# DeltaNet and SwiGLU on one core: where a chunk's first gate/value product stands, and which engine issues the output stores

## Chip, core and metric

The kernel runs on one core of a Trainium2 chip. The metric is the device time of one execution in microseconds (us). All arithmetic is in fp32.

The engines named below are TensorE (PE in the profile; PEld is its weight load), VectorE (DVE), ScalarE (ACT), GpSimd (POOL) and SyncE (SP). SP does no arithmetic. It issues DMA transfers, and ACT can issue them too. Each engine runs its own instructions in the order in which they were emitted, and engines wait for one another by semaphores.

## What is computed

The reference chains two blocks. The first is a DeltaNet recurrence over 768 time steps for 4 batches and 8 heads of size 48; the second is a SwiGLU feed-forward layer on its output, with 3072 tokens, a model width of 384 and an inner width of 1536:

```python
for t in range(S):
    y[:, :, t] = einsum('bhd,bhde->bhe', q[:, :, t], state)
    v_old = einsum('bhde,bhd->bhe', state, k_n[:, :, t])
    state = state + beta_t * einsum('bhd,bhe->bhde', k_n[:, :, t], v[:, :, t] - v_old)
x = y.transpose(0, 2, 1, 3).reshape(B * S, H * D)
g, val = x @ w_gate, x @ w_val
out = (g * sigmoid(g) * val) @ w_out
```

`k_n` is k divided by its norm.

## The kernel before

**Tiling.** Time is cut into 12 chunks of 64 steps. A chunk has 64 steps of 4 batches, so 256 tokens for the feed-forward layer. For each chunk the heads' part (the recurrence: Gram matrices, a triangular inverse, four steps of `advance`) makes the tile `xts[c]`, the layer's input; the feed-forward part of chunk c then runs while the heads' part of chunk c + 1 is put in between in small pieces.

**Order.** The order is written out by hand: inside `manual_schedule` all five engines keep the order of emission. `point(c + 1)` is a *head visit*: it emits one piece of the heads' work, which is either a step of `advance`, a join of the inverse, or the Gram products of a later chunk. `fill(n)` emits some n us of VectorE work of the inverse, with now and then a ScalarE copy (line 698). `finish(c + 1)` emits what is still missing of the next chunk's `advance`, and `x_sums` emits four small VectorE sums of the new input.

**Two forms of the feed-forward layer.** Chunks 0 to 2 use plain products (`gate_val`, line 1009, and `output`, line 1038). Chunks 3 to 11 (`c >= FAST`, with `FAST = 3`) use a form with seven block products instead of eight, in three rounds per chunk (`gate_val_fast`, matmuls at line 928) and one `output_fast` (line 1125). It works in four PSUM banks, called `p_x`, `p_w`, `p_y` and `p_v`.

**How a round begins.** `begin` makes a first product into `p_x` on PE (eight matmul records in the trace) and copies it to `p_y` on ACT (line 945). Then a second product goes into `p_w`, with ACT copying `p_w` away (line 971), and a third product is accumulated onto `p_y`. That third product needs ACT's copy at line 945 to have ended. Then ACT copies `p_y` to `p_v` (line 974). For rounds 1 and 2 `begin` is emitted at the end of the round before. For round 0 it stands inside round 0, after the head visit that the loop over chunks emits at line 1439:

```python
point(c + 1)                         # head visit
if c >= FAST:
    for r in range(ROUNDS):
        gate_val_fast(c, r, fill)    # round 0: begin(0), then product(p_w ...)
```

**Stores.** Each half of a chunk's output lies in a tile `o_sb`, of which there are two, and is stored by two DMAs of 96 KB (line 1055). ACT issues them for chunks 0 to 2, SP for chunks 3 to 11. All other loads of this part of the kernel are issued by SP: k, q and v of later chunks (lines 136, 169, 183), and the kept sums of weights (line 941). The loads by `first_blocks` are emitted between the two `output` calls of chunk 1, after the store of its first half.

Of the kernel before, what the change touches and what calls it, by code (L numbers as in the profile page):

```python
# [20 lines left out]
def kernel(  # L21
# [25 lines left out]
    nc = tc.nc  # L47
# [21 lines left out]
    def ps_pair(name, tag):  # L69
# [3 lines left out]
    ffn_banks = [  # L73
        psum.tile([128, 512], FP32, name=f"ffn{i}", tag=f"ffn{i}", bufs=1)
        for i in range(4)
    ]
    taken = []

    def ps_ffn(shape, name, bank=None):
        if bank is None:  # L80
            taken.append(name)
            bank = (len(taken) - 1) % 4
        n = 1
        for m in shape[1:]:
            n *= m
        p = ffn_banks[bank][:, 0:n]
        return p if len(shape) == 2 else p.rearrange("p (x n) -> p x n", x=shape[1])
# [240 lines left out]
    kt, qt, a_sb, a_of, p_sb, xts = {}, {}, {}, {}, {}, {}  # L328
# [3 lines left out]
    def half_of(x):  # L332
        return slice(64 * x, 64 * x + 64)
# [522 lines left out]
    def new_h(c, f, at):  # L856
        hs[c, f] = hp[at].rearrange("p (i n) -> p i n", i=2)
# [5 lines left out]
    def units(t):  # L863
        return t.rearrange("p (u n) -> p u n", u=4)

    w_s = {1: units(hp[6]), 2: units(hp[7]), 4: units(p_places[0][:, 0:512])}
# [6 lines left out]
    x_t = const.tile([128, 3, 128], FP32, name="x_t")  # L873

    def w_pair(m, t, f):
        return (wg_sb, wv_sb)[m][:, t, 128 * f : 128 * f + 256].rearrange(
            "p (i n) -> p i n", i=2
        )
# [31 lines left out]
    def x_sums(c):  # L910
        if c < NCH and c not in summed and steps("advance", c) >= 4:
            summed.add(c)
            sums_of_x(c)

    ROUNDS = 3

    def gate_val_fast(c, r, fill):

        f1, f2 = 2 * r, 2 * r + 6
        x = xts[c]  # L920
        p_x, p_w, p_y, p_v = (
            units(ps_ffn([128, 512], "p_gate", bank)) for bank in range(4)
        )
        tok = slice(0, 128), slice(128, 256)

        def product(p, w, moving, start=False):
            for u in range(4):
                nc.tensor.matmul(  # L928
                    p[:, u], w(u), moving, start=start and u == 0, stop=True,
                    skip_group_check=True,  # L930
                )

        def plain(t, f):
            return lambda u: w_pair(u // 2, t, f)[:, u % 2]

        def summed_w(n):
            return lambda u: w_s[n][:, u]

        def next_sums(n):
            if c < NCH - 1 or r < ROUNDS - 1:  # L940
                nc.sync.dma_start(out=w_s[n], in_=kept[n, (r + 1) % ROUNDS])

        def begin(r):
            product(p_x, plain(0, 2 * r), x[:, 0, tok[0]], True)
            nc.scalar.copy(p_y, p_x)  # L945

        def silu(p, n):
            nc.scalar.activation(  # L948
                sil[:, n].rearrange("p (i n) -> p i n", i=2), p[:, 0:2], ACTF.Silu
            )  # L950

        def times(p, n, f, j):
            nc.vector.tensor_tensor(  # L953
                out=h_of(c, f, j),
                in0=sil[:, n].rearrange("p (i n) -> p i n", i=2),
                in1=p[:, 2:4],
                op=ALU.mult,
            )

        def combo_or_fill(n):  # L960
            if combos:
                combos.pop(0)()
                n -= 1.9
            fill(n)

        for f in (f1, f2):
            new_h(c, f, f // 2)
        if r == 0:
            begin(0)
        product(p_w, summed_w(1), x_t[:, 0], True)  # L970
        nc.scalar.copy(m5, p_w)
        next_sums(1)
        product(p_y, summed_w(2), x_t[:, 1])
        nc.scalar.copy(p_v, p_y)  # L974
        next_sums(2)
        product(p_x, plain(1, f1), x[:, 1, tok[0]])
        product(p_x, plain(2, f1), x[:, 2, tok[0]])
        plus(p_y, p_y, m5)
        product(p_v, plain(0, f2), x[:, 0, tok[1]])
        silu(p_x, 0)  # L980
        fill(1)
        times(p_x, 0, f1, 0)
        plus(p_w, p_v, m5)
        point_and_fill(c + 1, 3.4, combo_or_fill)
        product(p_y, summed_w(4), x[:, 1, tok[1]])
        next_sums(4)
        product(p_y, plain(2, f1), x[:, 2, tok[1]])
        silu(p_y, 1)
        times(p_y, 1, f1, 1)
        product(p_w, plain(2, f2), x[:, 2, tok[1]])  # L990
        silu(p_w, 0)
        times(p_w, 0, f2, 1)
        product(p_v, plain(1, f2), x_t[:, 2])
        product(p_v, plain(2, f2), x[:, 2, tok[0]])
        silu(p_v, 1)
        sums_of_h(c, f2)
        times(p_v, 1, f2, 0)
        if r < ROUNDS - 1:
            begin(r + 1)
        point_and_fill(c + 1, 5, combo_or_fill)  # L1000

    def gate_val(c, f, fill, within=None, behind=None):
# [49 lines left out]

    def store(c, bp, o_sb):
        for b in range(2):
            (nc.scalar if c < FAST else nc.sync).dma_start(
                out=out_v[2 * bp + b, c * C : (c + 1) * C],
                in_=o_sb[half_of(b)],
            )
# [3 lines left out]
    FAST = 3  # L1062
# [18 lines left out]
    def plus(out, a, b):  # L1081
        nc.vector.tensor_tensor(out=out, in0=a, in1=b, op=ALU.add)  # L1082
# [12 lines left out]
    def h_of(c, f, bp):  # L1095

        return hs[c, f][:, :, 128 * bp : 128 * bp + 128]
# [6 lines left out]
    def sums_of_h(c, f):  # L1104
        f1 = f - FH
        nc.vector.tensor_tensor(
            out=s_of(1, f1), in0=h_of(c, f1, 1), in1=h_of(c, f, 1), op=ALU.add
        )
        minus(s_of(2, f1), s_of(1, f1), h_of(c, f1, 0))
        minus(h_of(c, f1, 1), h_of(c, f1, 0), h_of(c, f1, 1))  # L1110
# [71 lines left out]
    def step(kind, fn, *args):  # L1182
        key = (kind, args or (1,))
        if key not in gens:
            gens[key] = [fn(*args), 0]
        next(gens[key][0], None)
        gens[key][1] += 1

    def steps(kind, *args):
        return gens.get((kind, args), (None, 0))[1]  # L1190
# [33 lines left out]
    def may_advance(c):  # L1224
        g = c // 2
        due = {0: 1, 1: 2 + 2 * (c % 2)}.get(g, 2)
        return steps("advance", c) > 0 or (c in p_sb and steps("join", g) >= due)
# [12 lines left out]
    def prep_step(c):  # L1240

        if first:
            first.pop(0)()
            return True
        for g in range(1, c // 2 + 2):
            late = g == 1 and (
                hold or steps("join", g) >= 2 and steps("advance", 2) < 4
            )
            if g in inverted and steps("join", g) < (4 if g == 1 else 2) and not late:
                step("join", join if g > 1 else join_1, *((g,) if g > 1 else ()))  # L1250
                return True
        if going:
            next(going.pop())
            return True
        k_c, q_c = None, None
        if q_of and steps("advance", q_of[0] - 1) >= 3:
            q_c = q_of.pop(0)
        elif not (c > 0 and hold and not todo and k_ready()):
            return False
        if k_ready():  # L1260
            k_c = k_of.pop(0)
        gen = products(k_c, q_c)
        next(gen)
        going.append(gen)
        return True

    def point_and_fill(c, n, fill):
        spent.clear()
        point(c)
        n -= sum(spent)  # L1270
        if n > 0:
            fill(n)

    def point(c):

        mine = c < NCH and steps("advance", c) < 4 and may_advance(c)
        if mine and steps("advance", c) > 0:
            step("advance", advance, c)
        elif not prep_step(c - 1) and mine:
            step("advance", advance, c)  # L1280
# [12 lines left out]
    def fill(n):  # L1293
        if todo:

            filled.append(n)
            converts(2 if len(filled) < 4 else 1)
            if len(filled) == 1:
                converts(1)
        else:  # L1300
            after_weights()
            fill_some(n)
# [14 lines left out]
    with tc.manual_schedule(  # L1317
# [118 lines left out]
        output(1, 1, fill, range(2, FT, 2))  # L1436
        finish(2)
        for c in range(2, NCH):
            point(c + 1)
            if c >= FAST:  # L1440
                for r in range(ROUNDS):
                    gate_val_fast(c, r, fill)
                output_fast(c, fill)
            else:
                for f in range(0, FT, 2):
                    gate_val(c, f, fill, behind=c + 1)
                output(c, 0, fill)
                point(c + 1)
                output(c, 1, fill)
            finish(c + 1)  # L1450
            x_sums(c + 1)
# [30 lines left out]
```

## Time and profile before

| what | value |
|---|---|
| time, three executions | 719.43, 721.98 and 723.44 us; median 721.98 |
| profiled execution | 720.38 us, span 718.7 us |
| PE busy | 683.1 us, 95% of the span |
| DVE, ACT, POOL busy | 464.2, 254.9, 51.9 us (65%, 35%, 7%) |
| mean granted TensorE clock | 0.967 of full speed |
| chain that ended last, by engine | PE 85%, DVE 6%, ACT 3%, issue 2%, DMA 1%, POOL 1% |
| output stores issued by ACT | 12, of 0.47 to 0.61 us each |
| output stores issued by SP | 36 |

The busy time says how full an engine is over the whole span. The chain of waits is followed back from the last instruction and says which engine the end waited for at each moment. For an engine that is nearly always busy, the useful view is that of its few idle stretches: where they are, and what ended each. An idle stretch of another engine costs nothing while this one works.

In timeline rows the columns are start, length, engine, line, operation, output and inputs, and the count of merged instructions. In square brackets stands the idle time before, with what ended it. A letter q after an engine's name means its sequencer, which here issues DMAs.

### The profile page before, as it was taken

How to read it: one execution, taken by the hardware profiler on the slowest of the kernel's cores; microseconds unless marked ns; L12 is line 12 of the kernel's file. 1: busy time of each engine (PE TensorE's matmuls, PEld its weight loads, DVE VectorE, ACT ScalarE, POOL GpSimd, SP SyncE). 2: the span in 40 equal slices, each digit the busy share in tenths (PEclk: the TensorE clock that was granted, in tenths of full speed). 3: DMA queues.
4: the chain of work that ended last, by engine and by line, in shares of the span. 5: the costliest groups of instructions: out<-in, count | busy, mean ns of one | idle time of the engine just before them, and what ended most of it. 6: DMA issues, size and time to landing. Idle time of an engine off the chain costs nothing.

```text
span 718.7 us, 25292 instructions
## 1 busy us (share of the span) xinstructions
PE 683.1 (95%) x11212; PEld 629.3 (88%) x11212; DVE 464.2 (65%) x1052; ACT 254.9 (35%) x536; POOL 51.9 (7%) x46
## 2 busy tenths in 40 slices
PE   4757999999999999999999999999999999999997
PEld 3546788866788699999999999999999999999997
DVE  6995765777399477688756789559864435334342
ACT  3467755302331243243333234333053043142230
POOL 8003000203000003000030000300000000000000
PEclk9556999999999999999999999999999999999999
DMA  7786454221243134344434434134142222121211
GB/s 153 169 229 169 123 116 128 43 36 24 48 111 79 27 68 112 62 99 113 71 76 113 56 90 98 32 96 102 51 107 74 46 75 60 37 76 45 68 45 23
DMA packets 143278, 60.19 MB, mean 84 GB/s; under 512 B 124256, under 2 KB 127328, under 8 KB 143168
## 3 DMA queue, kind: packets, MB, share of 16 engines
q1 hardware_dynamic: 139712, 56.82, 33.8%
q10 hardware_dynamic: 3072, 1.57, 1.0%
q8 instruction: 88, 1.44, 0.8%
q0 software_dynamic: 384, 0.17, 0.1%
q14 instruction: 22, 0.18, 0.1%
HBM read 51.46 MB, written 7.08 MB: 81 GB/s over the span
## 4 chain that ended last, share of the span: by engine, by line
PE 85%; DVE 6%; ACT 3%; issue 2%; DMA 1%; POOL 1%; ACTq 0%; SPq 0%; DVEq 0%
PE ffn L928 36%; PE ffn L1125 16%; PE ffn L1009 13%; PE ffn L1038 6%; PE p_g L447 2%; DVE tmp L519 2%; DVE zb L525 2%; PE p_u L775 2%; PE p_r L753 2%; PE p_s L806 1%; PE p_y L794 1%; PE p_y L762 1%; DMA kn<-in_k_dram 1%; PE p_f L840 1%; POOL n_t L363 1%
## 5 line engine op out<-in xcount | busy, mean ns | idle before, releaser
L928 PE MATMUL ffn<-x_ffn,wg_sb 128*128 128x128 f32 x756 | 116.2, 276 | 0.3 <-DVE ffn L1082 0.3
L928 PE MATMUL ffn<-x_ffn,wv_sb 128*128 128x128 f32 x756 | 115.3, 275 | 0.0
L928 PEld LDWEIGHTS ffn<-x_ffn,wg_sb 128*128 128x128 f32 x756 | 99.6, 192 | 0.9 <-DVE ffn L1082 0.5
L928 PEld LDWEIGHTS ffn<-x_ffn,wv_sb 128*128 128x128 f32 x756 | 99.6, 192 | 0.0
L948 ACT ACTIVATE sil<-ffn 128x256 f32<-128x256 f32 x108 | 41.5, 385 | 122.5 <-PE ffn L928 117.0
L953 DVE TENSOR_TENSOR h_f<-sil,ffn 128x256 f32<-128x256 f32 x108 | 44.6, 418 | 48.7 <-ACT sil L948 46.8
L1125 PE MATMUL ffn<-wo_sb,h_f 128*128 128x192 f32 x432 | 75.2, 327 | 0.0
L1082 DVE TENSOR_TENSOR ffn<-ffn,p_sb 128x512 f32<-128x512 f32 x54 | 37.7, 697 | 53.3 <-ACT ffn L974 52.3
L1125 PEld LDWEIGHTS ffn<-wo_sb,h_f 128*128 128x128 f32 x432 | 70.3, 190 | 0.3
L525 DVE TENSOR_TENSOR zb<-zb,tmp 128x31 f32<-128x31 f32 (+15 forms) x186 | 63.8, 343 | 6.4
L519 DVE TENSOR_TENSOR tmp<-zb,mb 128x31 f32<-128x31 f32 (+15 forms) x186 | 63.3, 340 | 5.1
L928 PE MATMUL ffn<-x_t,h_f 128*128 128x128 f32 x432 | 54.6, 279 | 2.0 <-ACT ffn L945 2.0
L1009 PE MATMUL ffn<-x_ffn,wg_sb 128*128 128x256 f32 x216 | 53.2, 398 | 1.9 <-ACT x_ffn L843 1.9
L928 PEld LDWEIGHTS ffn<-x_t,h_f 128*128 128x128 f32 x432 | 50.9, 191 | 2.9 <-ACT ffn L945 2.3
L1009 PE MATMUL ffn<-x_ffn,wv_sb 128*128 128x256 f32 x216 | 49.9, 380 | 0.0
L661 POOL TENSOR_TENSOR n_b<-mb,half 128x32 f32<-128x32 f32 x5 | 28.0, 5596 | 303.2 <-DVE mb L489 264.1
L1009 PEld LDWEIGHTS ffn<-x_ffn,wg_sb 128*128 128x128 f32 x216 | 41.6, 198 | 8.5 <-ACT x_ffn L843 2.4
L1082 DVE TENSOR_TENSOR o_sb<-o_sb,ffn 128x192 f32<-128x192 f32 x45 | 15.8, 352 | 51.3 <-PE ffn L1125 44.3
L1038 PE MATMUL ffn<-wo_sb,h_f 128*128 128x384 f32 x136 | 45.7, 490 | 0.0
L1009 PEld LDWEIGHTS ffn<-x_ffn,wv_sb 128*128 128x128 f32 x216 | 40.7, 190 | 5.5
L1038 PEld LDWEIGHTS ffn<-wo_sb,h_f 128*128 128x128 f32 x136 | 25.3, 190 | 16.5
L945 ACT COPY ffn<-ffn 128x512 f32<-128x512 f32 x27 | 15.4, 571 | 56.6 <-PE ffn L928 47.9
(229 smaller groups left out, 1040.4 us busy)
## 6 DMA issues: line engine op xcount, KB each, us to landing
h_f<-w_s SPq DMA_DIRECT2D x52, 256.0 KB
p_sb<-w_s SPq DMA_DIRECT2D x26, 256.0 KB
vin<-in_v_dram SPq DMA_DIRECT2D x96, 48.0 KB
kn<-in_k_dram SPq DMA_DIRECT2D x40, 96.0 KB
out_dram<-o_sb SPq DMA_DIRECT2D x36, 96.0 KB
zt<-in_moe_w_out_dram SPq DMA_DIRECT2D x6, 384.0 KB
qpad<-in_q_dram SPq DMA_DIRECT2D x36, 64.0 KB
wo_sb<-in_moe_w_gate_dram SPq DMA_DIRECT2D x4, 512.0 KB
```

The lines of the kernel that those rows point to most:

```text
L447: nc.tensor.matmul(p_v[par][half_of(b if of_q else b ^ par), bp, j], kt[c][half_of(par), bp, j, b], xt[half_of(par), bp, j, b],)
L519: nc.vector.tensor_tensor(out=t_v, in0=zb[:, 0 : j + 1, j : j + 1].to_broadcast([128, j + 1, m]), in1=mb[:, j : j + 1, j + 1 : R].to_broad ...
L525: nc.vector.tensor_tensor(out=zb[:, 0 : j + 1, j + 1 : R], in0=zb[:, 0 : j + 1, j + 1 : R], in1=t_v, op=ALU.add,)
L661: nc.gpsimd.tensor_tensor(out=n, in0=mb.rearrange("p j i -> p (j i)")[:, 0 : R * R : R + 1], in1=half, op=ALU.pow,)
L928: nc.tensor.matmul(p[:, u], w(u), moving, start=start and u == 0, stop=True, skip_group_check=True,)
L945: nc.scalar.copy(p_y, p_x)
L948: nc.scalar.activation(sil[:, n].rearrange("p (i n) -> p i n", i=2), p[:, 0:2], ACTF.Silu)
L953: nc.vector.tensor_tensor(out=h_of(c, f, j), in0=sil[:, n].rearrange("p (i n) -> p i n", i=2), in1=p[:, 2:4], op=ALU.mult,)
L1009: nc.tensor.matmul(ps[name][:, i], w_sb[:, t, (f + i) * 128 : (f + i + 1) * 128], xts[c][:, t], start=(t == 0 and (i == 0 or c < 2)), stop ...
L1038: nc.tensor.matmul(p_o, hs[c, f - f % 2][:, f % 2, bp * 128 : (bp + 1) * 128], wo_sb[:, f], start=(f == 0), stop=(f == FT - 1),)
L1082: nc.vector.tensor_tensor(out=out, in0=a, in1=b, op=ALU.add)
L1125: nc.tensor.matmul(p[x, part], a(f - f % 2)[:, f % 2], b(f), start=not begun and f == 0, stop=f == FH - 1, skip_group_check=True,)
```

## The change

Two things are changed. First, `begin` of round 0 is emitted before the head visit that opens a chunk instead of after it; for that its helpers move out of `gate_val_fast`. The aim is that ACT's copy at line 945 no longer queues behind the ACT work of the head visit, and that it runs while PE works on the visit. Second, all output stores are issued by SP, so that ACT does not spend its own time on issuing those of chunks 0 to 2.

```diff
+    p_x, p_w, p_y, p_v = (units(bank) for bank in ffn_banks)
+    tok = slice(0, 128), slice(128, 256)
...
+    def begin(c, r):
+        product4(p_x, plain(0, 2 * r), xts[c][:, 0, tok[0]], True)
+        nc.scalar.copy(p_y, p_x)
...
-        def begin(r):
-            product(p_x, plain(0, 2 * r), x[:, 0, tok[0]], True)
-            nc.scalar.copy(p_y, p_x)
...
-        if r == 0:
-            begin(0)
-        product(p_w, summed_w(1), x_t[:, 0], True)
+        product4(p_w, summed_w(1), x_t[:, 0], True)
...
         if r < ROUNDS - 1:
-            begin(r + 1)
+            begin(c, r + 1)
...
     def store(c, bp, o_sb):
         for b in range(2):
-            (nc.scalar if c < FAST else nc.sync).dma_start(
+            nc.sync.dma_start(
...
         for c in range(2, NCH):
+            if c >= FAST:
+                begin(c, 0)
             point(c + 1)
             if c >= FAST:
                 for r in range(ROUNDS):
```

More of the change, by code (lines that the diff above doesn't have):

```diff
@@ L915, with product4, plain, summed_w @@
     ROUNDS = 3
+    p_x, p_w, p_y, p_v = (units(bank) for bank in ffn_banks)
+    tok = slice(0, 128), slice(128, 256)
+    def product4(p, w, moving, start=False):
+        for u in range(4):
+            nc.tensor.matmul(
+                p[:, u], w(u), moving, start=start and u == 0, stop=True,
+                skip_group_check=True,
+            )
+    def plain(t, f):
+        return lambda u: w_pair(u // 2, t, f)[:, u % 2]
+    def summed_w(n):
+        return lambda u: w_s[n][:, u]
+    def begin(c, r):
+        product4(p_x, plain(0, 2 * r), xts[c][:, 0, tok[0]], True)
+        nc.scalar.copy(p_y, p_x)
     def gate_val_fast(c, r, fill):
@@ L920, in gate_val_fast @@
         x = xts[c]
[L921 to L937, printed above, removed]
         def next_sums(n):
@@ L967, in gate_val_fast @@
             new_h(c, f, f // 2)
-        if r == 0:
-            begin(0)
-        product(p_w, summed_w(1), x_t[:, 0], True)
+        product4(p_w, summed_w(1), x_t[:, 0], True)
         nc.scalar.copy(m5, p_w)
         next_sums(1)
-        product(p_y, summed_w(2), x_t[:, 1])
+        product4(p_y, summed_w(2), x_t[:, 1])
         nc.scalar.copy(p_v, p_y)
         next_sums(2)
-        product(p_x, plain(1, f1), x[:, 1, tok[0]])
-        product(p_x, plain(2, f1), x[:, 2, tok[0]])
+        product4(p_x, plain(1, f1), x[:, 1, tok[0]])
+        product4(p_x, plain(2, f1), x[:, 2, tok[0]])
         plus(p_y, p_y, m5)
-        product(p_v, plain(0, f2), x[:, 0, tok[1]])
+        product4(p_v, plain(0, f2), x[:, 0, tok[1]])
         silu(p_x, 0)
@@ L984, in gate_val_fast @@
         point_and_fill(c + 1, 3.4, combo_or_fill)
-        product(p_y, summed_w(4), x[:, 1, tok[1]])
+        product4(p_y, summed_w(4), x[:, 1, tok[1]])
         next_sums(4)
-        product(p_y, plain(2, f1), x[:, 2, tok[1]])
+        product4(p_y, plain(2, f1), x[:, 2, tok[1]])
         silu(p_y, 1)
         times(p_y, 1, f1, 1)
-        product(p_w, plain(2, f2), x[:, 2, tok[1]])
+        product4(p_w, plain(2, f2), x[:, 2, tok[1]])
         silu(p_w, 0)
         times(p_w, 0, f2, 1)
-        product(p_v, plain(1, f2), x_t[:, 2])
-        product(p_v, plain(2, f2), x[:, 2, tok[0]])
+        product4(p_v, plain(1, f2), x_t[:, 2])
+        product4(p_v, plain(2, f2), x[:, 2, tok[0]])
         silu(p_v, 1)
```

## The prediction, as written before the changed kernel ran

> **What bounds the kernel now.** I read the busy shares first, then the table by stage, then PE's own waits, and last the timelines around each wait.
>
> ```profile
> PE 683.1 (95%) x11212; PEld 629.3 (88%) x11212; DVE 464.2 (65%) x1052; ACT 254.9 (35%) x536; POOL 51.9 (7%) x46
> ```
>
> ```profile
> 145.00:190.00 45.00, 43.95 (x690) 28.61 (x689) 30.53 (x68) 9.63 (x18) 7.17 (x3) 1.00 0.19 35
> 190.00:247.00 57.00, 57.00 (x804) 44.98 (x803) 43.86 (x111) 13.60 (x26) 0.00 (x0) 1.00 0.28 68
> 247.00:309.00 62.00, 60.04 (x1206) 58.41 (x1192) 40.07 (x79) 24.08 (x51) 6.58 (x3) 1.00 0.39 78
> 309.00:719.00 410.00, 405.26 (x6320) 397.95 (x6319) 245.59 (x565) 125.92 (x269) 13.16 (x6) 1.00 0.31 72
> ```
>
> The columns are the stretch, its length, the busy time of PE, PEld, DVE, ACT and POOL, then granted clock, DMA share and GB/s. From 145 us on PE is the bound. ACT is under 40% busy in each of these stretches, so it costs time only where PE waits for one particular instruction of it. PE's waits from 246 us to the end are these (total us, times, longest):
>
> ```profile
> PE ffn L928 <- ACT ffn L945: 2.0, 2, 1.4
> PE ffn L928 <- DVE ffn L1082: 0.3, 1, 0.3
> ```
>
> So of nine chunks with a `begin` in round 0, only two show PE waiting for the copy at line 945. The last 410 us have almost nothing to give: 405.26 us are busy, and the rest is switching between tile shapes plus that one wait for DVE. The first of the two waits is in chunk 3; this is ACT's timeline there:
>
> ```profile
> 246.84 0.48 ACT L1046 COPY o_sb<-ffn 128x384 f32<-128x384 f32 x1 [5.42 <-PE ffn L1038]
> 247.34 1.12 ACTq L1055 DMA_DIRECT2D out_dram<-o_sb  x2
> 248.51 1.76 ACT L698 COPY zt<-zt 32x512 f32<-32x512 f32 x3 [1.20 <-issue]
> 250.29 0.60 ACT L722 ACTIVATE t<-p_j 128x512 f32<-128x512 f32 x1
> 250.79 0.59 ACT L945 COPY ffn<-ffn 128x512 f32<-128x512 f32 x1
> ```
>
> The copy PE needs is last in a row of five. Ahead of it stand two stores (1.12 us), three inverse copies, and one copy of the head visit (line 722). The second wait is in chunk 4:
>
> ```profile
> 304.23 0.59 ACT L473 COPY a_sb<-p_g 128x512 f32<-128x512 f32 x1 [6.65 <-PE p_g L447]
> 304.85 0.74 ACT L476 COPY a_sb<-p_g 32x256 f32<-32x256 f32 x2
> 305.60 0.59 ACT L473 COPY a_sb<-p_g 128x512 f32<-128x512 f32 x1
> 306.21 0.74 ACT L476 COPY a_sb<-p_g 32x256 f32<-32x256 f32 x2
> 306.98 0.57 ACT L945 COPY ffn<-ffn 128x512 f32<-128x512 f32 x1
> ```
>
> There it queues behind six Gram copies of the visit. A third wait, in chunk 1, concerns the stores alone. ACT issues them while the transposed input lies ready in PSUM, and PE stands:
>
> ```profile
> 187.22 1.15 ACTq L1055 DMA_DIRECT2D out_dram<-o_sb  x2
> 188.41 0.80 ACT L843 COPY x_ffn<-p_f 128x768 f32<-128x768 f32 x1 [1.22 <-PE p_f L840]
> ...
> 189.26 0.92 PE L1009 MATMUL ffn<-x_ffn,wg_sb 128*128 128x256 f32 x3 [0.96 <-ACT x_ffn L843]
> ```
>
> **What the Trainium skill says.** "Perfetto Trace Analysis", section "Per-engine timelines" (the DMA instruction of the hardware path), says the profiled length of a DMA issue runs from its semaphores being satisfied until the sequencer is free again. The trace agrees: after 247.34 + 1.12 = 248.46 ACT's next instruction starts at 248.51. "DMA: Bandwidth & Descriptors", section "Issuing engines are not separate DMA queues", says transfers started by different engines share the same 16 DMA engines, and another issuer saves only sequencer time. I therefore give no gain to data movement; no run here shows that yet. "TensorEngine Tiling (Array Packing)", section "Key Properties", says a change of tiling mode drains TensorE. By start times in the trace, the first Gram matmul after a 128x192 product comes 0.256 us after it, against 0.163 inside the product; 0.205 after a 128x128 product, against 0.112. So the switch costs 0.093 us either way.
>
> **Part 1, `begin` ahead of the visit.** Nothing is added or removed: nine times, eight matmul records (8 x 0.112 = 0.90 us of PE) and one 0.57 us ACT copy change place with a visit. The number of mode switches stays: output, visit, `begin` has two, and output, `begin`, visit has two. By the start-time differences above, the sum in chunk 4 is 0.256 + 0.148 + 0.112 before and 0.163 + 0.205 + 0.148 after, both 0.516 us.
>
> *Chunk 4.* The eight matmuls into `p_w` start at 306.02 and are 0.112 us apart, so the third product could start at 306.02 + 0.90 = 306.92; it starts at 307.60. The loss is **0.68 us**. Afterwards `begin` ends on PE some 2 us before the visit's Gram products do, ACT is idle (6.65 us before), and the copy is done long before PE asks. All 0.68 us go. The Gram copies start 0.9 us later and end near 308; the copies at lines 971 and 974 then follow by about 309.0, and the product that needs line 974 comes after 16 more matmul records, 307.8 + 1.8 = 309.6. It hides.
>
> *The other seven chunks.* In chunk 5 the copy at 945 starts 0.33 us after ACT ran idle; no wait shows on PE in chunks 5 to 11. I give them nothing. What they risk is the visit being 0.90 us later. Queued behind it on DVE is the subtraction at line 770, for which PE's next visit waits. In chunk 6 this subtraction starts at 417.62, ends at 418.57, and PE uses it at 420.4. It is DVE's inverse work that places it so late: PE finished its input at 413.9. A PE product 0.90 us later, at 414.8, is still 2.8 us ahead. Cost 0.
>
> **Part 2, stores by SP.** ACT is freed of 12 issues of 0.57 us, 6.9 us in all, but only two pairs stand before something PE waits for.
>
> *Chunk 1.* The transposes end at 186.75 + 0.87 = 187.62; the copy at 843 could start at about 187.69 instead of 188.41 and let PE go 0.72 us sooner. PE has other work until 188.30, so at most 0.96 us are there. I take **0.72**.
>
> *Chunk 3, with part 1.* Without stores ACT goes on to the three line-698 copies at 247.34 and ends them at 247.34 + 1.76 = 249.10; the line-945 copy is next and ends at 249.67. PE, with `begin`, visit and `p_w` in new order, is ready at 248.94 + 0.90 = 249.84, so the wait goes: **1.59 us** (251.43 - 249.84). Part 1 alone would save 0.50 (the copy takes line 722's start at 250.29 instead of 250.79), part 2 alone 1.17 (248.51 - 247.34); together they make 1.67, and the wait is the limit.
>
> *The other four store pairs* (155, 163, 170, 239 us): PE shows no wait on what follows them. 0.
>
> *What SP queues behind the stores.* SP used to run ahead: the 16 `first_blocks` loads were issued from 139.0 to 147.3. They are emitted after chunk 1's first store, whose tile is ready at 170.6, so they must now wait for it: two stores (1.15 us), then 16 issues of 0.52 to 0.65, that is 171.8 to at most 182.2. Their first reader is the DVE transpose at 204.75. Before that SP issues v loads (181.74 on), which slip 0.5 us at most. The trace does not show these loads' landing in this place. From the nearest row, DMA from issue to landing 4.0 us for a 21 KB load, the last lands near 186, or if it took three times as long, near 194. Slack 10 to 18 us: cost 0.
>
> **Sum:** 0.68 + 0.72 + 1.59 = **2.99 us** on PE, in stretches after which PE runs full to the end, so it carries through. DVE would swallow it if it never waited for PE between 303 and the wait for DVE at 339.5; but it waits 0.66 and 0.52 us for ACT's silu at 329.19 and 330.13, more than the 0.68 that chunk 4 gains.
>
> **From which level.** The four executions on record (719.43, 721.98, 723.44, 720.38) have a mean of 721.31, below the median of three. I start there: 721.31 - 2.99 = **718.3 us**, 0.5% below the median.
>
> **Rivals.**
> - *A: all three waits go* (0.68 chance): 718.3. It straddles the bound of 718.37, so the spread between executions decides; I split it 0.42 faster, 0.26 within.
> - *B: the chunk-3 wait is taken over by the line-698 copies* or by a PSUM bank still read, and chunk 4 gains half: 0.72 + 0.60 + 0.34 = 1.7 us, about 719.7. For it: the copy ends at 249.67, only 0.17 us before PE needs it. Against it: line 698 waits for nothing in the trace once the stores are gone. Chance 0.16, within.
> - *C: more goes*: the wait for DVE at 339.5 (0.44 us) ends too, as DVE's work falls differently, and chunk 1 gives its full 0.96: 2.99 + 0.44 + 0.24 = 3.7, so 717.6. For it: both are PE waits that the trace shows. Against it: DVE works without a pause from 330.5 to 339.4 in either order. Chance 0.09, faster.
> - *D: slower.* The later visits push DVE's subtraction so that PE waits in every chunk: at worst nine times 0.90 = 8.1 us less 2.99, so 726.4; or `first_blocks` lands after 204.75. For it: DVE is the next fullest engine (65%) and in chunk 6 it is late already. Against it: the 2.8 us of slack. Chance 0.07.
>
> Faster 0.42 + 0.09 = 0.51; slower 0.07; within, the rest, 0.42. The range is 715.6 (C less the half spread of the times, 2 us) to 721.6 (B plus the same); it leaves out D.
>
> **What would show it.** PE's waits after 246 us should list no line 945; ACT's copy at 945 in chunk 3 should end before the visit's line-722 copy starts; PE's wait at 189 us should fall below 0.3 us; SP's `first_blocks` loads should sit at 172 to 182 us with the DVE transpose still moving with PE. I am wrong if PE shows new waits for line 770 or line 1082, if the 945 copy waits for a DVE read of its bank, or if the waits go and the span does not shrink by about 3 us.

## The result, and the profile after

The changed kernel takes 717.11 us (median; 716.09 to 719.0), the kernel before 720.87 us (719.43 to 723.44) in the same comparison. The ratio is 0.9948 with a 95% interval of 0.9935 to 0.9961: **0.52% faster, 3.76 us**, with 2.8 to 4.7 us inside the interval. Timed again beside later experiments, the changed kernel gave 0.9948 once more (0.9928 to 0.9967), 717.96 against 721.28 us. The forecast was 718.3 us, from three waits that sum to 2.99 us.

The profiled execution has a span of 715.2 us. Line numbers moved a little: the products are line 922 (928 before), `begin`'s copy is line 935 (945), `output_fast` is line 1122 (1125), plain gate products are line 1006 (1009), and the VectorE sums of line 1082 are now line 1079. First the page's busy row:

```profile
PE 681.8 (95%) x11212; PEld 629.1 (88%) x11212; DVE 463.9 (65%) x1052; ACT 254.4 (36%) x536; POOL 51.7 (7%) x46
```

The instruction counts are the same, and the busy times nearly so: PE's is 1.3 us lower, 0.6 us of it in the first 60 us. So most of the gain has to come from idle stretches. In the table by stage (stretch, its length, then busy PE, PEld, DVE, ACT, POOL, granted clock, DMA share, GB/s) PE's column says where:

```profile
145.00:190.00 45.00, 44.72 (x694) 29.28 (x693) 30.58 (x68) 10.60 (x19) 7.17 (x3) 1.00 0.26 42
...
247.00:309.00 62.00, 62.00 (x1238) 60.57 (x1231) 42.54 (x86) 23.42 (x50) 6.58 (x3) 1.00 0.41 82
```

PE's busy time rose from 43.95 to 44.72 us in the first stretch and from 60.04 to 62.00, all of it, in the second. Of PE's own waits from 145 us to the end (total, times, longest) two are left, and the copy of `begin` is not among them:

```profile
PE ffn L922 <- DVE ffn L1079: 0.3, 1, 0.3
PE ffn L1006 <- ACT x_ffn L843: 0.2, 1, 0.2
```

ACT's timeline in chunk 3 shows the new order. The two stores are gone, and the copy (now line 935) stands ahead of the visit's line 722:

```profile
245.55 0.48 ACT L1043 COPY o_sb<-ffn 128x384 f32<-128x384 f32 x1 [6.59 <-PE ffn L1035]
245.92 1.75 ACT L698 COPY zt<-zt 32x512 f32<-32x512 f32 x3
247.59 0.57 ACT L935 COPY ffn<-ffn 128x512 f32<-128x512 f32 x1
248.18 0.60 ACT L722 ACTIVATE t<-p_j 128x512 f32<-128x512 f32 x1
```

In chunk 4 the copy runs before the visit's Gram copies begin:

```profile
301.44 0.57 ACT L935 COPY ffn<-ffn 128x512 f32<-128x512 f32 x1 [6.42 <-PE ffn L922]
302.56 0.59 ACT L473 COPY a_sb<-p_g 128x512 f32<-128x512 f32 x1 [0.55 <-PE p_g L447]
```

In chunk 1 the copy of the transposed input follows the output copy, with no store in between:

```profile
186.22 0.48 ACT L1043 COPY o_sb<-ffn 128x384 f32<-128x384 f32 x1
187.13 0.80 ACT L843 COPY x_ffn<-p_f 128x768 f32<-128x768 f32 x1 [0.43 <-PE p_f L840]
```

SP issues the `first_blocks` loads where the prediction put them (172 to 182 us), behind chunk 1's first store:

```profile
171.31 5.21 SPq L169 DMA_DIRECT2D qpad<-in_q_dram  x8
176.61 5.93 SPq L169 DMA_DIRECT2D qpad<-in_k_dram  x8
```

To see how much each place gave, I compare the times at which the same PE work starts in the two traces; the difference is called the offset below. The head visits serve as marks, since they keep their line numbers. Where `begin` now stands ahead of a visit, that mark is left out.

| place | offset, after - before, us | gain there |
|---|---|---|
| to 187 us | -0.52 | 0.52, all of it there at 140 us, before any changed instruction |
| chunk 1's wait for line 843 | -0.53 to -1.29 | 0.76 |
| chunk 3's wait for the copy | -1.29 to -2.76 | 1.47 |
| chunk 3, third round: reload of weight sums | -2.76 to -2.56 | -0.20 |
| chunk 4's wait for the copy | -2.56 to -3.34 | 0.78 |
| chunks 5 to 11 | -3.35 to -3.54 | 0.19 |

The places that the change touches sum to **3.0 us**. At 140 us both programs have run the same instructions; in the eleven other traces taken here the offset at that mark lies between -0.7 and +1.2 us, so the first 0.52 us is no effect of the change. A second trace of the changed kernel repeats 0.76, 1.47, 0.79 and 0.21 us at the four places and has no loss at the reload, so its places sum to 3.2 us.

### The profile page after: what moved, and what is told of

It reads as the page before. It is cut to its first block, busy times and chain, and to the rows that moved or that the text cites. A ratio compares the mean times of both kernels' runs of the same rounds, so it can differ in the third digit from the quotient of the medians.

```text
span 715.2 us, 25294 instructions
## 1 busy us (share of the span) xinstructions
PE 681.8 (95%) x11212; PEld 629.1 (88%) x11212; DVE 463.9 (65%) x1052; ACT 254.4 (36%) x536; POOL 51.7 (7%) x46
## 4 chain that ended last, share of the span: by engine, by line
PE 88%; DVE 5%; ACT 3%; issue 1%; POOL 1%; DMA 1%; SPq 0%; ACTq 0%; DVEq 0%
PE ffn L922 37%; PE ffn L1122 17%; PE ffn L1006 12%; PE ffn L1035 7%; PE p_g L447 3%; DVE tmp L519 2%; DVE zb L525 2%; PE p_u L775 2%; PE p_r L753 2%; PE p_s L806 2%; PE p_y L762 1%; PE p_y L794 1%; PE p_f L840 1%; POOL n_t L363 1%; PE p_j L639 1%
```

## Experiments

Three theories stood against each other; their letters are those of the experiments and not of the prediction's cases. **Theory Q**: the gain is three PE waits, each for one ACT instruction that queues behind others. **Rival M**: moving `begin` gains in every one of nine chunks. **Rival A**: what counts is that ACT no longer spends 6.9 us on issuing.

### `begin` alone

```diff
-            nc.sync.dma_start(
+            (nc.scalar if c < FAST else nc.sync).dma_start(
```

> Only begin is moved ahead of the visit; the stores of chunks 0 to 2 stay on ACT. Theory Q (the gain is three waits of PE, each for one ACT instruction that queues behind others): chunk 1's wait for line 843 stays at about 0.96 us; chunk 3's wait for the copy shrinks from 1.44 us to about 1.0 because the two stores and the line-698 copies still stand ahead of it; chunk 4's 0.68 us goes. Gain 0.5 + 0.7, with 0.3 for switches about 1.5 us, ratio 0.998. Rival M (moving begin saves PE time in every one of nine chunks, the stores matter little): gain about 3 us or more, ratio 0.995 to 0.996. Rival A (ACT's 6.9 us of issuing is what counts): no gain here, ratio 1.000.

Measured: 719.58 us, ratio 0.9974 (0.9965 to 0.9983), 1.9 us with 1.2 to 2.5 inside. PE's waits:

```profile
PE ffn L1006 <- ACT x_ffn L843: 0.9, 1, 0.9
PE ffn L922 <- ACT ffn L935: 0.5, 1, 0.5
```

Chunk 1's wait is whole, chunk 3's is cut to 0.5 us, chunk 4's is gone. By the marks chunk 3 gives 0.63 us and chunk 4 0.79. Theory Q's places hold, and so do its gains. The wait left in chunk 3 is half of the 1.0 us that I wrote there, in the main because the visit, now behind `begin`, takes longer: from first to last, the 128 matmul records of line 716 start over 1.36 us, against 1.10 before. In all nine traces with `begin`'s matmuls ahead of this visit it is 1.33 to 1.38; why stays open. Rival A, which expected nothing here, falls, and so does rival M, whose 0.995 to 0.996 lies outside the interval. In this execution PE lost 1.93 us more between chunk 1's wait and 207 us, to which I return below.

### Stores alone

```diff
-            if c >= FAST:
-                begin(c, 0)
             point(c + 1)
+            if c >= FAST:
+                begin(c, 0)
```

> Only the stores move to SP; begin of round 0 stands behind the visit as before. Theory Q: chunk 1's wait falls to 0.2 us (gain 0.75), chunk 3's wait for the copy falls from 1.44 to about 0.3 us (gain 1.2), chunk 4's wait of 0.5 to 0.7 us stays whole. Gain about 1.9 us, ratio 0.9974. Rival M: gain under 0.5 us. Rival A: the whole gain of 3.8 us, ratio 0.995.

Measured: 718.73 us, ratio 0.9962 (0.9951 to 0.9973). Chunk 1 gives 0.75 us and chunk 3 1.30 by the marks; chunk 4 gives nothing, and its wait stands in PE's list:

```profile
PE ffn L922 <- ACT ffn L935: 0.5, 1, 0.5
```

The marks sum to 2.07 us, as theory Q has it (1.9). The times say 2.7 us with 1.9 to 3.5 inside, which excludes rivals M (under 0.5) and, narrowly, A (3.8). In chunk 3 the halves give 0.63 and 1.30 us, together 1.93, while the whole change got 1.47: the wait is the limit, as forecast.

### `begin` ahead in chunks 3 and 4 only

```diff
-            if c >= FAST:
+            if FAST <= c < FAST + 2:
                 begin(c, 0)
             point(c + 1)
+            if c >= FAST + 2:
+                begin(c, 0)
```

> Stores on SP; begin stands ahead of the visit in chunks 3 and 4 alone, behind it in chunks 5 to 11. Theory Q: PE shows no wait for the copy anywhere, and from chunk 5 to the end at most 0.03 us a chunk are lost, 0.2 us in all: gain against before 3.3 us or more, ratio about 0.995. Rival M: 7/9 of what begin brings is lost, gain about 2.3 us, ratio 0.997.

Measured: 717.85 us, ratio 0.9954 (0.9936 to 0.9971); the interval holds both expectations, so the trace has to decide. Its offset to the kernel before (-0.69 us of it there at 140 us) is -3.33 us after chunk 4 and -3.32 at the last mark: chunks 5 to 11 give nothing with the old order, while in the changed kernel they give 0.19 us, 0.03 a chunk. Rival M is refuted as the source of the gain; a remainder of it is real and small.

### Matmuls ahead, copy behind

```diff
             if c >= FAST:
-                begin(c, 0)
+                product4(p_x, plain(0, 0), xts[c][:, 0, tok[0]], True)
             point(c + 1)
+            if c >= FAST:
+                nc.scalar.copy(p_y, p_x)
```

> Stores on SP; begin's matmuls stand ahead of the visit on PE, but ACT's copy of them behind the visit's ACT work. Theory Q (the copy's place in ACT's queue is what counts): chunk 4's wait of about 0.7 us comes back, and in chunk 3 about 0.2 us; gain against before about 2.6 to 2.8 us, ratio 0.9962. Rival P (it is the order on PE, so that the product is ready early): as the changed kernel, no wait for the copy, ratio 0.995.

Measured: 720.2 us, ratio 0.9985 (0.9975 to 0.9995). Theory Q's direction holds and rival P falls, but the loss against the changed kernel is more than twice what I expected. ACT's timeline in chunk 4 shows the copy (line 1440) behind the visit's Gram copies:

```profile
305.64 0.73 ACT L476 COPY a_sb<-p_g 32x256 f32<-32x256 f32 x2
306.40 0.57 ACT L1440 COPY ffn<-ffn 128x512 f32<-128x512 f32 x1
```

PE's timeline there has the product into `p_w` and then the one that waits:

```profile
304.45 1.16 PE L922 MATMUL ffn<-x_t,h_f 128*128 128x128 f32 x8
307.03 1.16 PE L922 MATMUL ffn<-x_t,h_f 128*128 128x128 f32 x8 [1.41 <-ACT ffn L1440]
```

By start times the second row begins 1.69 us after the last matmul of the first, against 0.11 us without a wait, so PE loses 1.58 us; before the change it lost 0.68. The difference is 0.9 us, the length of `begin`'s matmuls. They push the visit, the visit's ACT copies and so the copy of line 1440 back by as much. I had counted the wait that returns and not the visit's delay. So the PE half of the move, on its own, made chunk 4 0.89 us slower than before; the gain needs the copy ahead of the visit's ACT work. Chunk 3 gave 1.11 us here against 1.47, and chunk 5 lost 0.33 us.

### Only two of six store pairs on SP

```diff
-            nc.sync.dma_start(
+            (nc.scalar if (c, bp) in ((0, 0), (0, 1), (1, 0), (2, 0)) else nc.sync).dma_start(
```

> As the changed kernel, but of the six store pairs of chunks 0 to 2 four go back to ACT (both halves of chunk 0, the first halves of chunks 1 and 2); SP issues only the second halves of chunks 1 and 2. Theory Q (only the two pairs stand ahead of an ACT instruction for which PE waits): no PE wait comes back, ratio as the changed kernel, 0.995. Theory A (the time ACT gets free counts as such): 4 of 6 pairs, two thirds of the stores' 2 us, are lost, ratio 0.9965.

Measured: 717.86 us, ratio 0.9952 (0.9937 to 0.9967), beside 717.96 us of the changed kernel on the same chip. The interval just holds rival A's 0.9965, so the trace has to decide here too: the offset is 0.45 us both at 140 and at 187 us, across the first three pairs, and chunk 1's gain is 0.76 us as in the changed kernel. So the four pairs are worth nothing, and rival A falls also by its own test. PE's list has no ACT wait in chunks 3 and 4; it has another one:

```profile
PE ffn L922 <- DMA h_f<-w_s: 1.5, 2, 0.9
PE ffn L922 <- DVE ffn L1079: 0.3, 1, 0.3
```

This is the -0.20 us row of the table above. In chunk 3's third round PE needs weight sums that SP reloads behind 16 other loads. In this execution SP took 5.77 us for the last eight of them, and the reload was issued at 272.01 against PE's need at about 274.4. In the other traces those eight took 4.8 to 5.3 us, and the wait was 0 to 0.6 us. It varies between executions of one program: the changed kernel's second trace has none. By the marks it cost 1.79 us in this execution. It appears in five of the seven traces in which chunk 3 has the whole `begin` ahead and SP reloads, and in none of the five others with SP's reload, so the change may bring PE nearer to it. That stays open. In one of the five, the second profile of `begin` alone, the list puts 0.2 us down to DVE's line 770; as PE starts there at 276.77, 3.0 us after the reload's issue at 273.76, and here the first wait ends 3.0 us after the issue too, I count it as the reload's.

### `first_blocks` later still

```diff
-        first_blocks(True)
-        first_blocks(False)
         point(2)
         output(1, 1, fill, range(2, FT, 2))
+        first_blocks(True)
+        first_blocks(False)
```

> As the changed kernel, with the 16 first_blocks loads emitted after chunk 1's last store instead of ahead of its second output: on SP they start near 190 us instead of 171 us, and end near 201 us. Theory Q (that they wait for stores costs nothing, as their reader comes at 203.5 us): with a landing time of up to 2.5 us still no wait, or at most 1 us on DVE of which PE sees less; ratio 0.995 to 0.9965. Rival D (loads that slip behind stores are near the edge already, and part of the gain was lost there): every us that they slip beyond shows on PE, some 5 us or more, ratio over 1.001.

Measured: 718.17 us, ratio 0.9955 (0.9942 to 0.9969). SP's timeline has the loads, and DVE's the transpose that reads them:

```profile
189.33 5.17 SPq L169 DMA_DIRECT2D qpad<-in_q_dram  x8
194.60 5.20 SPq L169 DMA_DIRECT2D qpad<-in_k_dram  x8
```

```profile
204.69 1.23 DVE L424 STREAM_TRANSPOSE kt<-qpad 128x1024 f32<-128x1024 f32 x1
```

The last issue ends at 199.80, 17 us later than in the changed kernel, and the transpose starts with no idle time before it. Rival D of the prediction, in its form "the loads slip into their reader", had at least 17 us of slack.

### The clock after chunk 1's wait

In the trace of `begin` alone the granted TensorE clock was half of full speed from 190.25 to 193.66 us, right after PE's 0.9 us wait for line 843. (Taken over whole microseconds, this reads as 0.5 to 0.7.) Three more profiles were taken of kernels that keep that wait: two of the kernel before (723.28 and 721.69 us) and one of `begin` alone (720.1 us), each a single execution.

> The kernel before, profiled again. Question: after PE's wait of about 1 us for line 843 near 189 us, does the granted clock drop (as it did once, in the kernel with begin alone moved, to 0.5 to 0.6 from 190 to 194 us, which cost 1.9 us)? If the wait brings the drop each time: a drop here too. If it depends on the execution: clock 1.00 from 145 us on in most looks. The wait for the copy in chunk 3 should be 1.4 us and in chunk 4 0.5 us by every theory.

> The kernel before once more, for the same question: a drop of the granted clock near 190 us in this execution or not. Reloads of weight sums in chunk 3's third round: a wait of 0 to 1.6 us, as SP's issuing of the 16 loads ahead of them takes shorter or longer.

> The kernel with begin alone moved, profiled again: the wait of 1 us near 189 us as before; if its drop of the clock belongs to this order of work, it comes again, with PE 1.9 us later by 207 us; if it belonged to that execution, the clock stays at 1.00.

The two profiles of the kernel before, by stage, the first one with the drop (the clock is the third column from the right):

```profile
190.00:192.00 2.00, 1.51 (x4) 1.25 (x5) 0.00 (x0) 1.93 (x4) 0.00 (x0) 0.66 0.32 77
192.00:196.00 4.00, 4.00 (x16) 3.33 (x15) 0.00 (x0) 0.73 (x2) 0.00 (x0) 0.74 0.00 1
```

In slices of 1 us the first one shows that the 0.66 and 0.74 are means over a clock of one half and a full one:

```profile
191.00:192.00 1.00, 1.00 (x4) 0.82 (x3) 0.00 (x0) 0.95 (x3) 0.00 (x0) 0.50 0.02 3
193.00:194.00 1.00, 1.00 (x4) 0.73 (x4) 0.00 (x0) 0.00 (x0) 0.00 (x0) 0.50 0.00 0
194.00:195.00 1.00, 1.00 (x6) 0.90 (x5) 0.00 (x0) 0.00 (x0) 0.00 (x0) 0.97 0.00 0
```

The second:

```profile
190.00:192.00 2.00, 1.43 (x7) 1.28 (x8) 0.00 (x0) 1.93 (x4) 0.00 (x0) 1.00 0.37 96
192.00:196.00 4.00, 4.00 (x23) 3.26 (x25) 0.00 (x0) 0.82 (x2) 0.00 (x0) 1.00 0.00 0
```

From 192 to 196 us PE issues 16 matmuls in the first and 23 in the second, and by 207 us the first has lost 1.91 us against the original trace of before, the second 0.21. The third profile, of `begin` alone, shows no drop. So of five traces with the wait two have the drop, at 1.9 us each; of the eight without it (the changed kernel, that kernel again, and six experiments) none has. That is suggestive, but five against eight traces do not settle it. The clock records of all thirteen traces say more about the drop's form: the clock is 1.00 or 0.50, and between two changes lie 3.41 us or a multiple of it. Both drops are one such step, the one right behind the step that holds the wait. How long PE was busy in the step with the wait does not tell the cases apart: 2.35 and 2.44 us of 3.41 where the drop followed, 2.37, 2.39 and 2.43 us where it did not.

### Three more edits of the same kind

```diff
+        if (c, r) != (FAST + 1, 2):
             fill(1)
...
-                nc.sync.dma_start(out=w_s[n], in_=kept[n, (r + 1) % ROUNDS])
+                (nc.scalar if (c, r) == (FAST, 1) else nc.sync).dma_start(
+                    out=w_s[n], in_=kept[n, (r + 1) % ROUNDS]
+                )
...
-            nc.sync.dma_start(
+            (nc.scalar if (c, bp, b) == (NCH - 1, 0, 1) else nc.sync).dma_start(
```

> The changed kernel with three more edits of the same kind, each at a place where an engine's queue makes the end wait. One: the inverse's fill of some 1.5 us of DVE work ahead of the sum that PE waits for in chunk 4's third round is left to later fills; PE's wait for DVE of 0.44 us should go. Two: in chunk 3's second round the three reloads of kept weight sums are issued by ACT instead of SP, where 16 loads stand ahead of them; the small gaps of PE near 274 us, 0.2 us in sum, should go. Three: of the two DMAs of the very last store one is issued by ACT beside SP, so that the end comes one issue of 0.6 us sooner. Theory Q: 1.2 us below the changed kernel, ratio about 0.993 to the kernel before. Rival: another wait takes their place or the end is set by landing, ratio 0.995.

Measured: 716.99 us, ratio 0.994 (0.992 to 0.9959), against 717.96 us and 0.9948 of the changed kernel on the same chip. The intervals overlap, so it is lower but not told apart. From 190 us on PE's list is empty of DVE and DMA:

```profile
PE ffn L1009 <- ACT x_ffn L843: 0.2, 1, 0.2
```

By the marks 0.22 us are won at the reload against the first trace of the changed kernel, nothing against its second, and 0.54 at the DVE wait. From there to the last mark 0.08 us are lost, where the changed kernel wins 0.19; that the fill that was left out changes later visits is my guess. The way from the last matmul's start to the end of the span is 4.2 us against 4.5, so splitting the last store brought 0.27 us, about half of one issue.

## Why the prediction was right, step by step

**Direction, size and time: right.** 718.3 us was forecast and 717.11 measured. As a difference to the kernel before, 3.0 us was worked out on PE, 3.0 is in the trace, and 3.76 (2.8 to 4.7) in the times.

- *Chunk 1, 0.72 us:* 0.76. The choice to let ACT start at the transposes' end and not to take the whole 0.96 was the right one; 0.2 us of wait is left.
- *Chunk 3, 1.59 us:* 1.47. The copy ends at 247.59 + 0.57 = 248.16, before the `p_w` matmuls end, so case B (the line-698 copies take the wait over) did not come. The sum left out two things, by start times. The wait cost more than its own length: the second matmul record behind it starts 0.213 us after the first, where the usual step is 0.112, so 0.10 us more was there to win. And the visit behind `begin` starts its records over 1.33 us in place of 1.10, which takes 0.23 us away. 1.59 + 0.10 - 0.23 = 1.46.
- *Chunk 4, 0.68 us:* 0.78. The difference is the same 0.10 us behind the wait. These are PE's rows there before the change:

```profile
306.02 1.06 PE L928 MATMUL ffn<-x_t,h_f 128*128 128x128 f32 x8
307.60 1.16 PE L928 MATMUL ffn<-x_t,h_f 128*128 128x128 f32 x8 [0.52 <-ACT ffn L945]
```

- *Chunks 5 to 11, nothing:* 0.19 us. The shape switches come out even, as forecast: in chunk 5 the offset is -3.35 us ahead of `begin` and -3.35 again within the `p_w` product. The 0.03 us come at the third product, the one that needs the copy. Before, its second matmul record follows the first by 0.142 to 0.144 us in place of 0.112 in each of chunks 5 to 11; in the changed kernel that is gone in chunks 5 to 10, and chunk 11, which has no visit, keeps it. In all of these the late record starts 0.26 to 0.27 us after the copy's end, as the second record did in chunks 3 and 4. So I take it for the tail of the same wait, too short for the list of waits; that is inferred. The later visits cost nothing: the changed kernel shows no PE wait for line 770.
- *Four store pairs, nothing:* right, shown by putting them back on ACT.
- *SP's queue, nothing:* right, the loads could slip 17 us more.
- *The level of 721.31 us:* the comparison gave 720.87, and 721.3 in the later ones. Starting below the first median was right. Of the 1.2 us by which the measured time lies under the forecast, 0.4 is this level and 0.8 the gain.
- *Case C:* the DVE wait did not go by itself. It went only when the fill ahead of it was left out.
- *A wrong reading:* the prediction puts PE's idle time after 309 us down to shape switches and the DVE wait. PE's last matmul ends at 714.54, so 4.46 of those 4.74 us lie behind it, where the last output is summed and stored (0.3 of them past the end of the span). This cost the forecast nothing, as both kernels have the same 4.5 us from the last matmul's start to the end; but it is a place where something can be won, as the split last store shows.

That 2.99 and 3.0 agree so closely is in part luck: +0.10 and -0.12 us in chunks 4 and 3, and +0.19 and -0.20 us in chunks 5 to 11 and at the reload, nearly cancel.

**The rest of the times.** The times gained 0.7 us more than the three waits, though 3.0 us lies inside their interval of 2.8 to 4.7, so nothing more may be there. The clock drop could explain it, for 2/5 of 1.9 us is 0.76, but with five traces that share is not known. One result speaks against it, if weakly: `begin` alone keeps the wait, so it should gain nothing by the drop, and yet its times gained 1.9 us (1.2 to 2.5) where its two traces give 1.0 and 1.4 us from 207 us on. The Trainium skill ("TensorE: Matmul & The Clock Gate", section "What's actually happening") describes a throttle that judges PE's activity in a free-running window of some 3.4 us and grants half or all of the clock. The traces agree with the length and with the half: 0.50 for one step of 3.41 us. The page has the slow state come after an idle window of that length; here a drop followed a wait of 0.9 us, and the measurement decides. Whether the wait brings it stays open.

## What to carry to other kernels

When one engine is busy all the time, price a reordering by that engine's few waits, one by one, and by which instructions stand ahead of the awaited one in the other engine's queue; the other engine's total time said nothing here, as the four store pairs put back on ACT show. An issued store held ACT's queue for about the length of a copy (0.56 us against 0.57), so it belongs on an engine whose next instruction nobody waits for. Move both halves of a producer pair: in chunk 4 the matmuls moved ahead without their copy only delayed the work behind them.

## What the runs showed of the hardware that I had not expected

A PE wait of about 0.9 us was followed in two of five traces by one step of 3.41 us at half the clock, which cost twice the wait itself (1.9 us). Behind PE's waits in chunks 3 and 4 the second matmul record came 0.213 us after the first in place of 0.112, so taking such a wait away returned 0.10 us more than its length. And the same 16 loads took SP between 8.9 and 9.8 us to issue in different executions, and a reload queued behind them cost PE 0 to 1.8 us.
